# One visit's first product moved ahead of another's second pass, the first block's x put first in the queue, and a third of the attention loads issued by ScalarE

## The chip, the cores and the metric

The kernel runs on one core of a Trainium2 chip. The core has five engines that run their own instruction streams and wait for each other by semaphores: TensorE (PE; its weight loads are listed as PEld), VectorE (DVE), ScalarE (ACT), GpSimd (POOL) and SyncE (SP), which here only issues DMAs. Within one engine the instructions run in the order in which the program wrote them. The metric is the device time of one execution in microseconds (us); lower is better. The kernel before takes 867.36 us (median of 3 runs, 867.32 to 869.23).

## The reference

An attention over short bands, and behind it a mixture of four dense experts that all work on every row.

```python
B, H, S, D = 4, 8, 576, 64          # attention
scores = q @ k.T / sqrt(D)
# heads 0-3: keys within 32 positions back; heads 4-7: every 4th of the last 128
attn = softmax(masked scores); x = (attn @ v) -> (2304, 512)
# experts: E = 4, D = 512, F = 1024
p = probs / sum(probs)
out = sum over e of p[:, e] * (relu(x @ w1[e]) @ w2[e])
```

All inputs and the output are float32.

## The kernel before

**Attention.** The work is cut into groups of one batch, one pair of heads and three blocks of 64 queries. Batch 0 has 12 steps of one group, batches 1 to 3 have 6 steps each of two groups. A step's life is a pipeline over the loop `for n in range(len(steps) + LAG)`: `s_qk` (PE, tile `sc`) and `s_max` (DVE, tile `sm` and `nm`) in turn n, `s_sub` (POOL) and `s_exp` (ACT) one turn later, `s_sum` (DVE) and `s_norm` (POOL) two, `s_tr` (PE transposes into `pt`, then a copy to `pts`) three, `s_av` (PE, tile `po`, then ACT copies it into the row tile `xr`) four turns later. At the head of each turn `load_qk` and `load_v` issue the DMAs of groups to come; each has 6 buffers, so a load waits until the group six before it has been used. All of them stand in SP's queue, with the loads of the expert weights (`r`, lines 98 and 106).

**Experts.** A float32 operand is split into a rounded high part and a rest (`split`, lines 113 and 116: ACT writes the high part, POOL or DVE the rest), and a product takes three matmuls per 128 rows: high by high, rest by high, high by rest. A *visit* (u, m) is slice u of the experts' hidden columns (256 of them, 16 slices in all) on row block m (768 rows, 3 blocks; block 0 is batch 0 and the first third of batch 1; its x parts are made in two halves). In a visit the first layer is done in seven products instead of eight (a Strassen scheme): `mm1_a` makes A11 B11 and A12 B21, `mm1_b` makes S2 T2, S1 T1, S3 T3, S4 B22, A22 T4. The S are sums of weight blocks (POOL, `w1_sums`, tile `r`, lines 141 to 147, then split by `w1_late` into `g2h` and `g2l`), the T are sums of x blocks (DVE, `x_sums`, line 203, then split by `x_part` into `xh_...` and `xl_...`). A product is six matmuls of 384 columns into the bank `x` (`m1x` in the profile) or `y` (`m1y`). Their results pass through ACT and DVE (`s`, `u`, lines 418 to 441) to relu and split (`hh` by ACT at line 399, `hl` by DVE at line 405). `mm2` is the second layer: per 128 rows six matmuls of 512 columns into a tile `m`, two with `hl`, and DVE adds the result, weighted, to the accumulator (`acc`, line 486). It runs in two halves of 3 row tiles: half 1 uses h12 and h22 of this visit, half 0 uses h11 and h21.

**What sets the order.** The generator `experts` gives out PE's work piece by piece; up to 12 pieces are put between two turns of the attention. After each piece one or two items are taken from lists of small jobs (`queue`, `later`: splits, sums, x parts). `prepare` appends a job; `need` runs everything in a list up to the job that is asked for. The first visit (0, 0) is done without Strassen (`plain`): half 0 first, then it pauses until the attention has reached turn `OPEN` (20), then half 1. Until turn 14 (`START`) dummy matmuls (`wt`, line 671) fill in. The order of a visit's pieces in the kernel before is

```
mm1_b(this visit), mm2(this visit, half 1), mm1_a(next visit), mm2(this visit, half 0)
```

In the first 374 us attention and experts are mixed; after that only experts remain, with two buffers for each of `x` and `y` and four for `m` (before that one each and two).

Of the kernel before, what the change touches and what calls it, by code (L numbers as in the profile page):

```python
# [17 lines left out]
GB = 3  # L18
# [24 lines left out]
def kernel(  # L43
# [74 lines left out]
    def w1_split(u):  # L118

        r = raw1[u]  # L120
        gh = wp.tile([128, 3, 2, 128], F32R, tag="g1h", name="g1h", bufs=2)
        gl = wp.tile([128, 3, 2, 128], F32R, tag="g1l", name="g1l", bufs=2)
        a11, a12 = r[:, 0:2, 0:128], r[:, 2:4, 0:128]
        a21, a22 = r[:, 0:2, 128:256], r[:, 2:4, 128:256]
        for i, a in enumerate((a11, a12, a22)):
            split(gh[:, i], gl[:, i], a, nc.scalar, nc.gpsimd if u > 1 else nc.vector)
            a_op[u, ("A11", "A12", "A22")[i]] = (gh[:, i], gl[:, i])
            yield
        if u == 0:
            gh, gl = (wp.tile([128, 4, FU], F32R, tag=t, name=t) for t in ("g2h", "g2l"))  # L130
            v = (slice(None), slice(0, 2), slice(128, 256))
            split(gh[v], gl[v], a21, nc.scalar, nc.vector)
            a_op[u, "A21"] = (gh[v], gl[v])
# [86 lines left out]
    def attention(ap, xrp, pa):  # L220
# [27 lines left out]

        def load_v(b, p, gi):
            v_s = ap.tile([KB, 2, GB, 64], F32, tag="v", name="v_s", bufs=6)  # L250
            nc.sync.dma_start(out=v_s, in_=vw[b, p][:, :, gi * GB:(gi + 1) * GB, :])
            v_t[b, p, gi] = v_s

        def s_qk(n, gs):
# [67 lines left out]
        def s_tr(n, gs):  # L322
            sm = st[n]
            outs = []
            for k in range(len(gs)):
                pt = pa.tile([128, 512], F32, tag="pa", name="pt")
                for i in range(GB):
                    nc.tensor.transpose(  # L328
                        pt[:KB, i * 128:(i + 1) * 128], sm[:, k * GB + i, :KB], ident
                    )  # L330
                ts_ = ap.tile([KB, GB * 128], F32, tag="pts", name="pts", bufs=2)
                if k:
                    nc.vector.tensor_copy(ts_, pt[:KB, :GB * 128])
                else:
                    nc.scalar.activation(out=ts_, in_=pt[:KB, :GB * 128], func=AF.Copy)
                outs.append(ts_)
            st[n] = outs
# [75 lines left out]

    def mm1_a(k):
        u, m = k
        x, z, s1 = bank("x"), bank("y"), tmp("s1")
        product(x, u, "A11", m, "B11", True)
        nc.scalar.activation(out=s1, in_=x, func=AF.Copy)  # L418
        yield
        product(z, u, "A12", m, "B21", True)  # L420
        nc.vector.tensor_tensor(out=s1, in0=z, in1=s1, op=ALU.add)  # L421
        h_out(k, "11", s1, 2)
        st[k] = x
        yield
# [73 lines left out]
    def experts(begin):  # L498

        for half in range(2):  # L500
            for n in ("X12", "B22") if half else ("B11", "B21"):
                for i in range(2):
                    need(x_part, i, n)
            need(w1_split, 0)
            yield from plain((0, 0), half)
            if half == 1:
                for n, js in (("T4", (1, 0)), ("T3", (1,)), ("T1", (1,)), ("T2", (1,))):
                    for j in js:
                        prepare(x_part, j, n, soon=True)
                prepare(w1_late, 1, soon=True)  # L510
                prepare(w1_split, 2)
                prepare(w1_sums, 2)
            need(w2_late, 0)
            yield from mm2((0, 0), True, False, half)
            if half == 0:
                yield from pause("open")
            else:
                prepare(w2_late, 2)
        need(w1_split, 1)
        yield from mm1_a(visits[0])  # L520
        for i, (u, m) in enumerate(visits):
# [13 lines left out]
            if m == blocks[-1] and u + 2 <= LAST:  # L535
                prepare(w1_split, u + 2)
                prepare(w1_sums, u + 2)
            if m == blocks[0]:
                need(w2_late, u)
            yield from mm2((u, m), *ends, 1)  # L540
            if i + 1 < len(visits):
                begin()
                need(w1_split, visits[i + 1][0])
                need_x(visits[i + 1][1], ("B11", "B21"))
                yield from mm1_a(visits[i + 1])
                if visits[i + 1] == (NU - 1, 0):

                    need(x_sums, 5)
                    for n in ("T2", "T1"):
                        for j in (4, 5):  # L550
                            prepare(x_part, j, n)
# [30 lines left out]
    with tc.manual_schedule():  # L582
# [108 lines left out]
            when.setdefault(n, []).append((i, names))  # L691

        flat = [g for s in steps for g in s]
        qk_done = av_done = qk_next = v_next = 0

        dummies(18)
        ffn = experts(begin)
        for n in range(len(steps) + LAG):
# [14 lines left out]
                av_done += len(steps[n - LAG])  # L713
            for i, names in when.get(n, ()):
                for name in names:
                    of = queue if i < 2 else later
                    if name is None or name == "T2":
                        prepare(x_sums, i, of=of)
                    if name is not None:
                        prepare(x_part, i, name.upper(), of=of)  # L720
            if n == 6:
                fetch_w1(0)
            if n == 8:
# [92 lines left out]
```

## Time and profile before

| | |
|---|---|
| median of the runs | 867.36 us (3 runs) |
| the profiled execution's own time | 869.94 us |
| its span, first to last instruction | 868.2 us |
| mean granted TensorE clock | 0.987 of full speed |
| PE busy | 840.4 us (97%), 5096 matmul records |
| DVE, POOL, ACT busy | 504.9, 418.7, 328.4 us |
| chain that ended last, share of PE | 86% |

PE is busy 97% of the span, but its matmuls are pipelined and their ends modelled, so the gaps that are listed are a little shorter than what they cost. The table by stages in the rows below is to be read first: from 380 to 840 us PE never stands, and most of the 28 us in which it does lie before that. A row of the timeline gives the start, the duration and, in brackets, how long the engine had been idle before it and what released it.

### The profile page before, as it was taken

How to read it: one execution, taken by the hardware profiler on the slowest of the kernel's cores; microseconds unless marked ns; L12 is line 12 of the kernel's file. 1: busy time of each engine (PE TensorE's matmuls, PEld its weight loads, DVE VectorE, ACT ScalarE, POOL GpSimd, SP SyncE). 2: the span in 40 equal slices, each digit the busy share in tenths (PEclk: the TensorE clock that was granted, in tenths of full speed). 3: DMA queues.
4: the chain of work that ended last, by engine and by line, in shares of the span. 5: the costliest groups of instructions: out<-in, count | busy, mean ns of one | idle time of the engine just before them, and what ended most of it. 6: DMA issues, size and time to landing. Idle time of an engine off the chain costs nothing.

```text
span 868.2 us, 13457 instructions
## 1 busy us (share of the span) xinstructions
PE 840.4 (97%) x5096; PEld 733.1 (84%) x5096; DVE 504.9 (58%) x1046; ACT 328.4 (38%) x771; POOL 418.7 (48%) x491
## 2 busy tenths in 40 slices
PE   9697899999999999999999999999999999999998
PEld 6476688887888888888988989889898898988987
DVE  4677766568665568755455554555555555555454
ACT  4434544445344444533323422333333332333221
POOL 4557887677766678844323423422432332342210
PEclk9798999999999999999999999999999999999999
DMA  7862223322222211321001001010100100100003
GB/s 189 226 183 80 74 91 120 103 83 83 76 63 87 74 49 51 124 69 49 24 25 50 25 25 49 27 47 25 49 25 25 49 25 25 49 25 25 1 28 118
DMA packets 54528, 56.77 MB, mean 65 GB/s; under 512 B 5952, under 2 KB 43840, under 8 KB 54464
## 3 DMA queue, kind: packets, MB, share of 16 engines
q1 hardware_dynamic: 54464, 55.92, 21.0%
q8 instruction: 40, 0.66, 0.3%
q14 instruction: 24, 0.20, 0.1%
HBM read 51.19 MB, written 4.72 MB: 64 GB/s over the span
## 4 chain that ended last, share of the span: by engine, by line
PE 86%; DVE 7%; POOL 3%; ACT 2%; DMA 2%; issue 1%; SPq 0%; POOLq 0%; DVEq 0%; ACTq 0%
PE m L478 43%; PE m1x L381 22%; PE m1y L381 16%; DVE hl L405 3%; PE sc L263 1%; PE pt L328 1%; PE po L348 1%; DMA k_s<-kT 1%; DMA r<-w 1%; DVE xr L203 1%; DVE u L441 1%; PE wt L671 1%; DVE sm L277 1%; ACT hh L399 1%; ACT xh_T L113 0%
## 5 line engine op out<-in xcount | busy, mean ns | idle before, releaser
L486 DVE SCALAR_TENSOR_TENSOR acc<-m,pn,acc 128x512 f32<-128x512 f32 x270 | 201.8, 749 | 96.6 <-PE m L478 95.1
L478 PE MATMUL m<-w2h,hh 128*128 128x512 f32 x576 | 227.2, 394 | 3.2 <-DVE acc L486 2.5
L116 POOL TENSOR_TENSOR g2l<-r,g2h 128x256 fp32r<-128x256 f32 x124 | 92.7, 767 | 282.9 <-PE m L478 195.7
L478 PE MATMUL m<-w2l,hh 128*128 128x512 f32 x576 | 225.8, 392 | 0.0
L478 PE MATMUL m<-w2h,hl 128*128 128x512 f32 x576 | 182.4, 394 | 4.5 <-DVE hl L405 4.4
L478 PEld LDWEIGHTS m<-w2h,hl 128*128 128x128 f32 x576 | 108.0, 188 | 34.2 <-DVE hl L405 10.6
L478 PEld LDWEIGHTS m<-w2h,hh 128*128 128x128 f32 x576 | 108.1, 188 | 30.1 <-DVE acc L486 5.1
L478 PEld LDWEIGHTS m<-w2l,hh 128*128 128x128 f32 x576 | 108.2, 188 | 17.9
L116 POOL TENSOR_TENSOR w2l<-r,w2h 128x512 fp32r<-128x512 f32 x62 | 80.9, 1325 | 45.4 <-ACT w2h L113 45.2
L418 ACT ACTIVATE s<-m1x 128x384 f32<-128x384 f32 x47 | 23.1, 492 | 175.5 <-PE m1x L381 175.5
L437 DVE TENSOR_TENSOR s<-m1x,s 128x384 f32<-128x384 f32 x47 | 26.2, 558 | 103.9 <-PE m1x L381 102.6
L399 ACT ACTIVATE hh<-s 128x384 fp32r<-128x384 f32 x94 | 49.4, 526 | 98.1 <-DVE s L437 51.3
L116 POOL TENSOR_TENSOR g1l<-r,g1h 128x256 fp32r<-128x256 f32 x90 | 66.8, 757 | 36.2 <-ACT g1h L113 36.2
L430 ACT ACTIVATE u<-m1x 128x384 f32<-128x384 f32 x47 | 23.1, 492 | 146.8 <-PE m1x L381 146.8
L405 DVE SCALAR_TENSOR_TENSOR hl<-s,hh 128x384 fp32r<-128x384 f32 x94 | 59.6, 634 | 28.4 <-ACT hh L399 28.4
L421 DVE TENSOR_TENSOR s<-m1y,s 128x384 f32<-128x384 f32 x47 | 26.2, 557 | 61.1 <-PE m1y L381 58.3
L381 PE MATMUL m1x<-xh_T,g2h 128*128 128x384 f32 x156 | 52.8, 339 | 0.6 <-ACT u L430 0.3
L381 PE MATMUL m1x<-xl_T,g2h 128*128 128x384 f32 x156 | 52.6, 337 | 0.2 <-DVE xl_T L116 0.2
L381 PE MATMUL m1x<-xh_T,g2l 128*128 128x384 f32 x156 | 52.4, 336 | 0.0
L113 ACT ACTIVATE g2h<-r 128x256 fp32r<-128x256 f32 x125 | 45.2, 406 | 0.0
L381 PE MATMUL m1y<-xl_B,g2h 128*128 128x384 f32 x128 | 43.4, 339 | 0.0
L381 PE MATMUL m1y<-xh_B,g2h 128*128 128x384 f32 x128 | 43.4, 339 | 0.0
(92 smaller groups left out, 1584.8 us busy)
## 6 DMA issues: line engine op xcount, KB each, us to landing
r<-w SPq DMA_DIRECT2D x64, 512.0 KB, 3.5
v_s<-vw SPq DMA_DIRECT2D x48, 144.0 KB, 3.2
k_s<-kT SPq DMA_DIRECT2D x48, 112.0 KB, 3.1
q_s<-qT SPq DMA_DIRECT2D x48, 96.0 KB, 3.0
out<-acc SPq DMA_DIRECT2D x18, 256.0 KB, 2.0
mask<-masks SPq DMA_DIRECT2D x1, 288.0 KB, 2.9
pw<-probs SPq DMA_DIRECT2D x1, 36.0 KB, 4.5
```

The lines of the kernel that those rows point to most:

```text
L113: nc.scalar.activation(out=hi, in_=src, func=AF.Copy)
L116: lo_eng.tensor_tensor(out=lo, in0=src, in1=hi.bitcast(F32), op=ALU.subtract)
L203: nc.vector.tensor_tensor(out=quarter(i, d), in0=quarter(i, a), in1=quarter(i, b), op=ALU.subtract)
L381: nc.tensor.matmul(bank, w[:, k], x[:, k], start=(first and k == 0 and i == 0), stop=(last and k == 1 and i == 2), skip_group_check=True,)
L399: nc.scalar.activation(out=hi, in_=src, func=AF.Relu)
L405: nc.vector.scalar_tensor_tensor(out=lo, in0=src, scalar=0.0, in1=hi.bitcast(F32), op0=ALU.max, op1=ALU.subtract)
L418: nc.scalar.activation(out=s1, in_=x, func=AF.Copy)
L421: nc.vector.tensor_tensor(out=s1, in0=z, in1=s1, op=ALU.add)
L430: nc.scalar.activation(out=u2, in_=x, func=AF.Copy)
L437: nc.vector.tensor_tensor(out=s5, in0=x, in1=s5, op=ALU.add)
L478: nc.tensor.matmul(po, h, w, start=(n == 0 and x == 0), stop=(n == 3))
L486: nc.vector.scalar_tensor_tensor(out=acc, in0=po, scalar=pn[:, tt, e:e + 1], in1=acc, op0=ALU.mult, op1=ALU.add,)
```

## The change

It has five parts.

1. `load_v` of batches 0 and 1 is issued by ScalarE's queue instead of SyncE's (24 of 48 loads).
2. The copy of the second group's transposes (`pts`) is done by ACT instead of DVE in the six steps of batch 1.
3. The x parts of block 0 that a turn prepares are put at the head of the list `queue` instead of its end. With it, in half 1 of the first visit, the split and the sums of w1 slice 1 are called for before the T parts are prepared.
4. The rest parts of w1 slice 1 (`g1l`, three of them) are made by POOL instead of DVE.
5. `mm1_a` makes A12 B21 first (into `y`, ACT copies it), and A11 B11 after it (into `x`, DVE adds it). The next visit's A12 product is put ahead of this visit's `mm2` half 1, its A11 product stays behind it; the calls of `begin`, `need(w1_split)` and `need_x` move ahead with it.

```diff
--- before.py
+++ after.py
@@ -123,7 +123,7 @@
         a11, a12 = r[:, 0:2, 0:128], r[:, 2:4, 0:128]
         a21, a22 = r[:, 0:2, 128:256], r[:, 2:4, 128:256]
         for i, a in enumerate((a11, a12, a22)):
-            split(gh[:, i], gl[:, i], a, nc.scalar, nc.gpsimd if u > 1 else nc.vector)
+            split(gh[:, i], gl[:, i], a, nc.scalar, nc.gpsimd if u else nc.vector)
             a_op[u, ("A11", "A12", "A22")[i]] = (gh[:, i], gl[:, i])
             yield
         if u == 0:
@@ -248,7 +248,8 @@
 
         def load_v(b, p, gi):
             v_s = ap.tile([KB, 2, GB, 64], F32, tag="v", name="v_s", bufs=6)
-            nc.sync.dma_start(out=v_s, in_=vw[b, p][:, :, gi * GB:(gi + 1) * GB, :])
+            queue = nc.scalar if b < 2 else nc.sync
+            queue.dma_start(out=v_s, in_=vw[b, p][:, :, gi * GB:(gi + 1) * GB, :])
             v_t[b, p, gi] = v_s
 
         def s_qk(n, gs):
@@ -329,7 +330,7 @@
                         pt[:KB, i * 128:(i + 1) * 128], sm[:, k * GB + i, :KB], ident
                     )
                 ts_ = ap.tile([KB, GB * 128], F32, tag="pts", name="pts", bufs=2)
-                if k:
+                if k and gs[k][0] > 1:
                     nc.vector.tensor_copy(ts_, pt[:KB, :GB * 128])
                 else:
                     nc.scalar.activation(out=ts_, in_=pt[:KB, :GB * 128], func=AF.Copy)
@@ -413,12 +414,13 @@
 
     def mm1_a(k):
         u, m = k
-        x, z, s1 = bank("x"), bank("y"), tmp("s1")
+        z, s1 = bank("y"), tmp("s1")
+        product(z, u, "A12", m, "B21", True)
+        nc.scalar.activation(out=s1, in_=z, func=AF.Copy)
+        yield
+        x = bank("x")
         product(x, u, "A11", m, "B11", True)
-        nc.scalar.activation(out=s1, in_=x, func=AF.Copy)
-        yield
-        product(z, u, "A12", m, "B21", True)
-        nc.vector.tensor_tensor(out=s1, in0=z, in1=s1, op=ALU.add)
+        nc.vector.tensor_tensor(out=s1, in0=x, in1=s1, op=ALU.add)
         h_out(k, "11", s1, 2)
         st[k] = x
         yield
@@ -504,6 +506,8 @@
             need(w1_split, 0)
             yield from plain((0, 0), half)
             if half == 1:
+                need(w1_split, 1)
+                need(w1_sums, 1)
                 for n, js in (("T4", (1, 0)), ("T3", (1,)), ("T1", (1,)), ("T2", (1,))):
                     for j in js:
                         prepare(x_part, j, n, soon=True)
@@ -535,14 +539,18 @@
             if m == blocks[-1] and u + 2 <= LAST:
                 prepare(w1_split, u + 2)
                 prepare(w1_sums, u + 2)
+            if i + 1 < len(visits):
+
+                begin()
+                need(w1_split, visits[i + 1][0])
+                need_x(visits[i + 1][1], ("B11", "B21"))
+                opening = mm1_a(visits[i + 1])
+                yield next(opening)
             if m == blocks[0]:
                 need(w2_late, u)
             yield from mm2((u, m), *ends, 1)
             if i + 1 < len(visits):
-                begin()
-                need(w1_split, visits[i + 1][0])
-                need_x(visits[i + 1][1], ("B11", "B21"))
-                yield from mm1_a(visits[i + 1])
+                yield from opening
                 if visits[i + 1] == (NU - 1, 0):
 
                     need(x_sums, 5)
@@ -691,6 +699,7 @@
             when.setdefault(n, []).append((i, names))
 
         flat = [g for s in steps for g in s]
+        first_x = []
         qk_done = av_done = qk_next = v_next = 0
 
         dummies(18)
@@ -713,11 +722,13 @@
                 av_done += len(steps[n - LAG])
             for i, names in when.get(n, ()):
                 for name in names:
-                    of = queue if i < 2 else later
+                    of = first_x if i < 2 else later
                     if name is None or name == "T2":
                         prepare(x_sums, i, of=of)
                     if name is not None:
                         prepare(x_part, i, name.upper(), of=of)
+            queue[:0] = first_x
+            first_x.clear()
             if n == 6:
                 fetch_w1(0)
             if n == 8:
```

**SyncE and ScalarE in the single-group steps** (q_s, k_s, v_s are the load buffers, r1 the raw w1 slice, xr, pts and sm the attention tiles). SyncE before:

```order
L245 DMA q_s_281<-qT 128x192
L246 DMA k_s_282<-kT 128x224
L251 DMA v_s_285<-vw 96x2x192
L245 DMA q_s_322<-qT 128x192
L246 DMA k_s_323<-kT 128x224
L251 DMA v_s_326<-vw 96x2x192
L245 DMA q_s_362<-qT 128x192
L246 DMA k_s_363<-kT 128x224
L251 DMA v_s_366<-vw 96x2x192
L98 DMA r1_400<-w1 128x4x256
```

SyncE in the change, at the same place:

```order
L245 DMA q_s_281<-qT 128x192
L246 DMA k_s_282<-kT 128x224
L245 DMA q_s_322<-qT 128x192
L246 DMA k_s_323<-kT 128x224
L245 DMA q_s_362<-qT 128x192
L246 DMA k_s_363<-kT 128x224
L98 DMA r1_400<-w1 128x4x256
```

The v loads of the same groups stand in ScalarE's queue in the change, each ahead of the copies of its turn:

```order
L302 ACTIVATE sm0_94<-sm0_94 128x3x96
L252 DMA v_s_326<-vw 96x2x192
L365 ACTIVATE xr_299<-po_333 128x4x48
L336 ACTIVATE pts_345<-pt_341 96x384
L302 ACTIVATE sm1_95<-sm1_95 128x3x96
L252 DMA v_s_366<-vw 96x2x192
L365 ACTIVATE xr_299<-po_373 128x4x48
L336 ACTIVATE pts_385<-pt_381 96x384
```

SyncE has two issues per group where it had three, and ScalarE one more in each turn.

**ScalarE at the start of half 1 of the first visit** (turn 20; xh_T4 from xr_930 and xh_B22 are the second halves of the x parts that this half multiplies, xh_T2, T1, T3 are for the visit after it, g1h, w2h and g2h are weight splits of slice 1). Before:

```order
L113 ACTIVATE xh_T2_0_1278<-xr_299 128x2x192
L113 ACTIVATE xh_T1_0_1282<-xr_299 128x2x192
L113 ACTIVATE xh_T3_0_1286<-xr_299 128x2x192
L113 ACTIVATE g1h_1290<-r1_617 128x256 x3
L113 ACTIVATE w2h_1302<-r2_683 128x512 x2
L113 ACTIVATE xh_T4_0_883<-xr_930 128x2x192
L113 ACTIVATE xh_B22_0_887<-xr_930 128x2x192
L399 ACTIVATE hh_1337<-m1x_1315 128x384
L399 ACTIVATE hh_1348<-m1y_1316 128x384
```

In the change:

```order
L113 ACTIVATE xh_T4_0_883<-xr_930 128x2x192
L113 ACTIVATE xh_B22_0_887<-xr_930 128x2x192
L400 ACTIVATE hh_1305<-m1x_1283 128x384
L400 ACTIVATE hh_1316<-m1y_1284 128x384
L113 ACTIVATE xh_T2_0_1320<-xr_299 128x2x192
L113 ACTIVATE xh_T1_0_1324<-xr_299 128x2x192
L113 ACTIVATE xh_T3_0_1328<-xr_299 128x2x192
L113 ACTIVATE g1h_1332<-r1_617 128x256 x3
L113 ACTIVATE w2h_1344<-r2_683 128x512
L113 ACTIVATE g2h_1356<-r1_617 128x2x128 x4
```

The two x parts have moved from behind eight copies to the front, and those copies now stand behind the two `hh`, which wait for the products of this half. POOL takes its work at this place from those copies; in the change its order is

```order
L116 TENSOR_TENSOR xl_T2_0_1321<-xr_299,xh_T2_0_1320 128x2x192
L116 TENSOR_TENSOR xl_T1_0_1325<-xr_299,xh_T1_0_1324 128x2x192
L116 TENSOR_TENSOR xl_T3_0_1329<-xr_299,xh_T3_0_1328 128x2x192
L116 TENSOR_TENSOR g1l_1333<-r1_617,g1h_1332 128x256 x3
L141 TENSOR_TENSOR r1_617<-r1_617 128x2x128
L143 TENSOR_TENSOR r1_617<-r1_617 128x2x128
L145 TENSOR_TENSOR r1_617<-r1_617 128x2x128
L147 TENSOR_TENSOR r1_617<-r1_617 128x2x128
L116 TENSOR_TENSOR w2l_1345<-r2_683,w2h_1344 128x512
L116 TENSOR_TENSOR g2l_1357<-r1_617,g2h_1356 128x2x128 x4
```

where before the row of the three `g1l` is missing (DVE made them) and both `w2l` stand ahead of `g2l`.

**TensorE at the end of a visit on block 0** (m1x and m1y are the banks x and y, g1h and g1l the split of A22 and then of A12, m2 the second layer). Before:

```order
L381 MATMUL m1x_1590<-xh_T4_0_883,g1h_1419 128x384
L381 MATMUL m1x_1590<-xh_T4_0_883,g1l_1420 128x384
L381 MATMUL m1x_1590<-xl_T4_0_884,g1h_1419 128x384
L478 MATMUL m2_1796<-w2h_1571,hh_1775 128x512
L478 MATMUL m2_1796<-w2l_1572,hh_1775 128x512
L478 MATMUL m2_1796<-w2h_1571,hh_1780 128x512
L478 MATMUL m2_1796<-w2l_1572,hh_1780 128x512
L478 MATMUL m2_1796<-w2h_1571,hl_1778 128x512
L478 MATMUL m2_1796<-w2h_1571,hl_1782 128x512
```

In the change:

```order
L382 MATMUL m1x_1599<-xl_T4_0_884,g1h_1428 128x384
L382 MATMUL m1y_1796<-xh_B21_0_739,g1h_1656 128x384
L382 MATMUL m1y_1796<-xh_B21_0_739,g1l_1657 128x384
L382 MATMUL m1y_1796<-xl_B21_0_740,g1h_1656 128x384
L480 MATMUL m2_1806<-w2h_1580,hh_1775 128x512
L480 MATMUL m2_1806<-w2l_1581,hh_1775 128x512
L480 MATMUL m2_1806<-w2h_1580,hh_1780 128x512
L480 MATMUL m2_1806<-w2l_1581,hh_1780 128x512
L480 MATMUL m2_1806<-w2h_1580,hl_1778 128x512
L480 MATMUL m2_1806<-w2h_1580,hl_1782 128x512
```

Six matmuls of the next visit (three rows, each twice) have come between the last product of this visit and the matmul that reads `hl`; the number of matmuls is the same.

## Rows read from the trace of the kernel before

**Rows 1.** Busy time of each engine by stretch, with granted clock and DMA share

```profile
core 0: us, PE busy (x) PEld busy (x) DVE busy (x) ACT busy (x) POOL busy (x), PEclk, DMA share, GB/s
...
32.00:40.00 8.00, 4.83 (x47) 3.12 (x47) 4.39 (x28) 3.52 (x8) 6.00 (x6) 0.59 0.78 225
40.00:48.00 8.00, 7.00 (x54) 6.07 (x57) 2.02 (x14) 0.56 (x2) 2.25 (x2) 0.56 0.85 253
...
100.00:380.00 280.00, 271.88 (x1744) 233.82 (x1743) 183.93 (x356) 128.48 (x312) 207.79 (x231) 1.00 0.26 83
380.00:840.00 460.00, 460.00 (x2304) 415.20 (x2303) 239.99 (x384) 148.28 (x336) 150.90 (x187) 1.00 0.10 32
```

**Rows 2.** Waits of PE: us in total, times, longest us

```profile
PE m1x L381 <- ACT xh_T L113: 4.6, 2, 4.4
PE m L478 <- DVE hl L405: 4.4, 10, 0.5
PE sc L263 <- DMA k_s<-kT: 3.6, 3, 2.5
...
PE po L348 <- DVE pts L333: 0.3, 1, 0.3
```

**Rows 3.** Timeline of SP's DMA issues: start us, us, what

```profile
12.81 1.61 SPq L251 DMA_DIRECT2D v_s<-vw  x1
...
16.25 0.54 SPq L245 DMA_DIRECT2D q_s<-qT  x1
16.83 0.43 SPq L246 DMA_DIRECT2D k_s<-kT  x1
17.30 0.57 SPq L251 DMA_DIRECT2D v_s<-vw  x1
```

**Rows 4.** Timeline of all engines, 24 to 42 us; idle before and releaser in brackets

```profile
29.73 0.63 ACT L113 ACTIVATE w2h<-r 128x512 fp32r<-128x512 f32 x1 [1.33 <-DMA r<-w]
...
31.01 0.57 PE L348 MATMUL po<-pts,v_s 96*64 96x64 f32 x12 [0.80 <-ACT pts L335]
...
32.53 0.53 PE L328 MATMUL pt<-ident,sm 128*96 128x128 f32 x3 [0.95 <-POOL sm L316]
```

**Rows 5.** Timeline of all engines, 12 to 20 us: ScalarE's copies of one turn

```profile
15.90 0.33 ACT L364 ACTIVATE xr<-po 128x192 f32<-128x192 f32 x1 [0.48 <-PE po L348]
...
16.41 0.49 ACT L335 ACTIVATE pts<-pt 96x384 f32<-96x384 f32 x1 [0.18 <-PE pt L328]
```

**Rows 6.** Timeline of all engines, 134.5 to 140.5 us: a visit's end

```profile
136.21 0.34 PE L381 MATMUL m1x<-xh_T,g1h 128*128 128x384 f32 x1
...
136.41 0.56 DVE L441 TENSOR_TENSOR u<-m1y,u 128x384 f32<-128x384 f32 x1 [0.41 <-PE m1y L381]
...
137.28 0.39 PE L478 MATMUL m<-w2h,hh 128*128 128x512 f32 x1
...
137.91 1.09 DVE L405 SCALAR_TENSOR_TENSOR hl<-u,hh 128x384 fp32r<-128x384 f32 x1
...
138.20 0.40 PE L478 MATMUL m<-w2h,hl 128*128 128x512 f32 x1
...
139.06 0.50 PE L478 MATMUL m<-w2h,hl 128*128 128x512 f32 x1 [0.47 <-DVE hl L405]
```

**Rows 7.** Timeline of ACT, 56 to 96 us

```profile
69.58 1.33 ACT L113 ACTIVATE xh_T<-xr 128x384 fp32r<-128x384 f32 x3
```

**Rows 8.** Timeline of PE, 60 to 100 us

```profile
73.33 0.69 PE L381 MATMUL m1x<-xh_T,g1h 128*128 128x384 f32 x1 [4.35 <-ACT xh_T L113]
...
87.53 0.44 PE L381 MATMUL m1x<-xh_T,g2h 128*128 128x384 f32 x1 [0.25 <-ACT xh_T L113]
```

**Rows 9.** Timeline of POOL, 56 to 96 us

```profile
70.16 3.09 POOL L116 TENSOR_TENSOR xl_T<-xr,xh_T 128x384 fp32r<-128x384 f32 x3
73.95 0.97 POOL L141 TENSOR_TENSOR r<-r 128x256 f32<-128x256 f32 x1 [0.70 <-DVE g1l L116]
...
77.91 2.83 POOL L116 TENSOR_TENSOR w2l<-r,w2h 128x512 fp32r<-128x512 f32 x2
80.97 2.17 POOL L116 TENSOR_TENSOR g2l<-r,g2h 128x256 fp32r<-128x256 f32 x3 [0.23 <-ACT g2h L113]
```

## The prediction

> **What bounds the kernel now.** I read the busy time by stages first. From 380 to 840 us PE is busy 460.00 of 460 us; from 100 to 380 us 271.88 of 280 [rows 1]. Nothing that the change does to the late stage can shorten it, unless it adds a wait: the matmuls are the same in number. What can be had lies in the gaps of the first 380 us, so I read PE's waits second, sorted by total. Three sums matter: 4.6 us for an x part from ACT (nearly all of it one wait of 4.35 us), 4.4 us in ten waits for `hl` from DVE, and 3.6 us in three waits for a k load [rows 2]. Third, the granted clock: 0.59 and 0.56 in the stretches 32 to 40 and 40 to 48 us [rows 1], so much of that stretch ran at 1.2 GHz instead of 2.4, after PE had stood repeatedly between 31 and 34 us [rows 4]. The change has a part for each of these.
>
> **Part 1, v loads from ScalarE.** In the single-group steps SP spends 0.54 + 0.43 + 0.57 us on the three issues of a group, and with the gaps a group takes it from 16.25 to about 17.98, so 1.73 us [rows 3]. Nothing waits on SP there except the loads themselves, but there is no room for the four weight loads and the table of probabilities, and some issues take longer (1.61 us at 12.81). Without v a group costs it about 1.0 us. The k loads that PE waited for should then be in time. I count the whole 3.6 us [rows 2]. The w2 load, which stands behind them on SP, also comes earlier: ACT waited 1.33 us for it, and behind that wait stood the copy that PE's `po` at 31.01 missed (0.80 us idle) and, by way of POOL, the `pt` at 32.53 (0.95) [rows 4]. I count both, 1.75 us. The lower end of these two sums is nothing at all, or a little below nothing, if the early q, k and mask loads now share the transfer engines with three v loads issued beside them; I allow 1 us.
>
> What it costs: each issue sits on ACT. In a turn ACT is idle 0.48 us before the `xr` copy and 0.18 us before `pts` [rows 5], together 0.66, against one issue of 0.57 us as on SP [rows 3]. It just fits, so I cost it at nothing, but with 0.09 us of room. If the issue must wait for an older transfer, `xr`, `pts` and the exponential queue behind it, and PE's next `po` waits for `pts`. That is a rival below.
>
> The Trainium skill speaks against this part: its page "DMA: Bandwidth & Descriptors", section "Issuing engines are not separate DMA queues", says that loads started from different engines run on the same 16 DMA engines, and that only the time to start them is saved, usually small beside the transfer. Here that time is not small, since three issues fill 1.73 us per group; but the DMA share of 0.78 to 0.85 from 32 to 48 us [rows 1] says that the engines have little room either. By the rule the 3.6 and 1.75 us would stay.
>
> **The clock.** From 32 to 48 us PE is busy 4.83 + 7.00 us at mean clocks of 0.59 and 0.56 [rows 1]. A mean of 0.59 between the two levels is (1 - 0.59) / 0.5 = 82% of the time at the low one, 0.56 is 88%. So 0.82 x 4.83 + 0.88 x 7.00 = 10.1 us of PE's work ran at half speed, and 5.0 us would be saved if it ran at full speed. Whether the clock stays up depends on the gaps that are left between 24 and 34 us, of which part 1 removes some. And some of the gain would be given back: a faster PE meets the attention's chain on DVE and POOL, which had time then (DVE 2.02 of 8 us busy from 40 to 48). Between 0 and 5.0 I take 2.5.
>
> **Part 2, `pts` by ACT.** One copy less on DVE in six steps. By the list PE waited 0.3 us for it in all (`po` for DVE's `pts`) [rows 2]; I count that, from 0 to 1.
>
> **Parts 3 and 4, block 0's x first.** The wait of 4.35 us ends when the x part of half 1 arrives at 73.33 [rows 8]. ACT began its row of x copies at 69.58, but with T parts and weight splits for the next visit [rows 7]. With the two parts in front PE could start near 70.2, that is 3.1 us earlier. But the eight copies that were in front are now behind two `hh`, and these wait for the products of half 1. I follow POOL, which has to make what comes next. Half 1's 24 first-layer matmuls take four times 1.07 us (a product from 136.21 to 137.28 [rows 6]), to 74.5; two `hh`, then the first T copy on ACT, to 75.5. From there POOL's order is three `xl_T` (3.09), three `g1l`, which DVE made before (2.17, as three `g2l` of the same size), four sums (73.95 to 77.91, so 3.96), one `w2l` (half of 2.83) and the first `g2l` (0.72) [rows 9]: 11.4 us, to 86.9. S2 T2, the first product of the next visit that needs this `g2l`, began at 87.53 before [rows 8]. So of 3.1 us only 0.6 is left there, because the chain on POOL ran under the long wait and now starts after it. PE would arrive near 81.2 (75.0, then 18 matmuls of the second layer at 0.23, then two products) and stand over 5 us, longer than the 4.35 us after which the clock fell last time, so the fall moves with it. On the other side the T parts are further ahead, and two or three short waits behind 87.53 go. I count 0, from -3 (clock low over more work) to 4.4 (the whole wait gone).
>
> **Part 5, A12 ahead.** In the visits on block 0 PE reads `hl` as the fifth matmul of half 1. The five from 137.28 to 138.20 start 0.23 apart, the next at 139.06: 0.63 us lost (0.47 listed as idle) since `hl<-u` began at 137.91 and took 1.09 [rows 6]. There are ten of these [rows 2], so 6.3 us. The A12 product puts 1.07 us between, more than any of them, and `hl` needs nothing from it. What can it wait for itself? Bank y: the add at 136.41 that reads it ends at 136.97, 0.3 us before A12 would start at 137.28 [rows 6]. And its weight split, which stands one visit ahead in the lists. A11's result is added by DVE instead of copied by ACT, then has the 4 us of half 0 before x is written again. I count 6.3, from 0 to 7.
>
> **The sum.** 3.6 + 1.75 + 2.5 + 0.3 + 0 + 6.3 = 14.45 us. The profiled execution took 869.94 us (span 868.2 and 1.74 around it), 2.58 above the median of the runs, 867.36. Its gaps are taken to be the median's too, so the change comes to 867.36 - 14.45 = 852.9, say **853 us**. Nothing after 380 us takes it back, as PE has no idle time there in which to lose it.
>
> **Rivals.**
> - *The transfers come no earlier* (the shared DMA engines bound them). For: DMA share of 0.85. Against: 225 and 253 GB/s in those stretches [rows 1] while SP is what feeds them. Parts 1 and the clock give nothing; 0.3 + 6.3 = 6.6 is left: 860.8 us.
> - *The opening pays too.* The 4.35 us wait goes without a new one, if POOL's chain is shorter than the sum above or the splits are not late: 14.45 + 4.4 = 18.9, 848.5 us. Against: POOL's order, which the change itself lays down.
> - *A12 meets bank y or a late split*, and the ten waits only change their name: 14.45 - 6.3 = 8.15, 859.2 us. Against: 0.3 us of room at 136.97.
> - *ScalarE is held by the loads, slower.* The place is ACT's queue in the 18 steps of batches 0 and 1. It decides from an issue that takes more than the 0.66 us of idle time per turn. An issue like SP's of 1.61 us is 0.95 too long; in 15 of the 18 steps that is 14.2 us, with the low clock at the opening (3) 17.2, against the 6.6 that parts 2 and 5 give: +10.6, 878 us. Against: SP's ordinary issue is 0.57.
>
> **How the numbers follow.** The forecast has 0.59, transfers no earlier 0.15, the opening pays 0.13, A12 waits 0.07, ScalarE held 0.06. Forecast's own range, from the clock (2.5 either way) and the opening: 848 to 858. For 8 in 10 the range takes in the first two rivals: **846 to 862**. A measurement of this kernel can tell 0.3%, 2.6 us. Faster by more than that: the first four, 0.94, less 0.05 for sums of several low ends that come out at nothing: 0.89. Same 0.05. Slower 0.06.
>
> **What would show it.** Right: no wait of PE for k loads, the clock at 1.00 from 32 to 48 us, half 0's first m1 matmul 5 to 8 us earlier than in the kernel before; no wait of `m` for `hl` from 100 to 374 us; the first matmul of half 1 less than 1.5 us after the attention's last, and a new wait of 4 to 6 us before the first `g2h` product, with POOL busy through it. Wrong: ACT idle behind a v issue with `pts` late; a wait of m1y for `u`; PE idle after 380 us.

## The result and the profile after

The changed kernel takes 858.99 us (median of 4 runs, 857.71 to 859.81) against 867.34 us for the kernel before (median of 4, 866.63 to 869.23): a ratio of 0.9891, 95% interval 0.9868 to 0.9914, so 9.5 us less by the ratio (7.5 to 11.4) and 8.35 us less by the medians. The forecast was 853 us, 14.45 less. The direction was right. The time is inside the range of 846 to 862, but outside the forecast's own 848 to 858: the gain is 58% of what was summed by the medians, 66% by the ratio. The profiled execution took 858.22 us, with a span of 856.4.

The busy times by stages (columns as in [rows 1]) show where it came from:

```profile
32.00:40.00 8.00, 6.61 (x96) 5.39 (x97) 6.99 (x44) 3.88 (x10) 6.58 (x7) 1.00 0.83 257
40.00:48.00 8.00, 7.44 (x100) 6.07 (x99) 6.36 (x34) 5.19 (x12) 6.52 (x7) 1.00 0.67 178
72.00:80.00 8.00, 2.77 (x14) 2.11 (x14) 2.69 (x4) 2.84 (x8) 7.69 (x10) 0.94 0.00 0
80.00:100.00 20.00, 19.47 (x126) 17.07 (x126) 13.39 (x30) 11.11 (x28) 18.16 (x19) 0.85 0.29 89
300.00:320.00 20.00, 17.93 (x82) 15.68 (x81) 10.32 (x16) 8.63 (x21) 13.49 (x15) 0.91 0.20 58
380.00:840.00 460.00, 460.00 (x2300) 416.14 (x2299) 242.22 (x384) 144.58 (x330) 148.21 (x184) 1.00 0.10 33
```

From 32 to 48 us the clock is at 1.00 in this execution, where it was 0.59 and 0.56 [rows 1], and the late stage is untouched. Two places are worse than they should be: PE is busy 2.77 of 8 us from 72 to 80, and from 300 to 320 us there is a new hole of 2.07 us with a lower clock behind it. The list of PE's waits (us in total, times, longest) names both:

```profile
PE m1x L382 <- DVE s L423: 4.9, 1, 4.9
PE m L480 <- DVE acc L488: 3.0, 2, 1.7
PE pt L329 <- POOL sm L317: 2.7, 4, 1.2
PE m1y L382 <- DVE hl L406: 2.1, 1, 2.1
...
PE m1x L382 <- ACT xh_T L113: 1.1, 1, 1.1
```

Of the three sums of [rows 2], the k loads are gone, the ten waits of `m` for `hl` are gone, and the 4.35 us for the x part is 1.1. In their place stand 4.9 us for an `s` of DVE and 2.1 us of `m1y` for `hl`. The first is the wait that the forecast had put before the first `g2h` product. In the timeline of PE (start, duration, idle before and releaser):

```profile
62.47 0.44 PE L382 MATMUL m1x<-xh_T,g1h 128*128 128x384 f32 x1 [1.13 <-ACT xh_T L113]
...
79.81 0.66 PE L382 MATMUL m1x<-xh_T,g2h 128*128 128x384 f32 x1 [4.94 <-DVE s L423]
80.26 0.52 PE L382 MATMUL m1x<-xh_T,g2l 128*128 128x384 f32 x1
```

and POOL through it, beside DVE's adds and x parts:

```profile
68.28 2.96 POOL L116 TENSOR_TENSOR xl_T<-xr,xh_T 128x384 fp32r<-128x384 f32 x3 [5.89 <-ACT xh_T L113]
71.20 2.12 POOL L116 TENSOR_TENSOR g1l<-r,g1h 128x256 fp32r<-128x256 f32 x3
73.40 0.74 POOL L141 TENSOR_TENSOR r<-r 128x256 f32<-128x256 f32 x1
...
77.73 3.74 POOL L116 TENSOR_TENSOR g2l<-r,g2h 128x256 fp32r<-128x256 f32 x4
```

```profile
77.56 0.63 DVE L116 TENSOR_TENSOR xl_T<-xr,xh_T 128x384 fp32r<-128x384 f32 x1 [4.55 <-ACT xh_T L113]
78.35 0.84 DVE L116 TENSOR_TENSOR xl_T<-xr,xh_T 128x384 fp32r<-128x384 f32 x1 [0.15 <-ACT xh_T L113]
79.11 0.55 DVE L423 TENSOR_TENSOR s<-m1x,s 128x384 f32<-128x384 f32 x1
```

```profile
75.78 1.33 ACT L113 ACTIVATE g2h<-r 128x256 fp32r<-128x256 f32 x4 [5.32 <-POOL r L145]
```

POOL idles 5.89 us under half 1 and then works almost without a gap; its first `g2l` ends near 78.7. DVE's add that frees the bank x stands behind two T parts, whose copies on ScalarE stand behind the `g2h` copies, and these wait for POOL's sums. Both ways come out of the same chain. The distance from the start of the wait before half 1 to S2 T2 is 79.81 - (62.47 - 1.13) = 18.47 us; before it was 87.53 - (73.33 - 4.35) = 18.55 [rows 8]. The opening gave nothing, as forecast; that two effects cancel there is shown below, where parts 3 and 4 are undone.

### The profile page after: what moved, and what is told of

Read it like the earlier page. It is cut to its first block, busy times and chain, and to the rows that moved or that the text cites. A ratio compares the mean times of both kernels' runs of the same rounds, so it can differ in the third digit from the quotient of the medians.

```text
span 856.4 us, 13489 instructions
## 1 busy us (share of the span) xinstructions
PE 833.1 (97%) x5096; PEld 735.0 (86%) x5096; DVE 501.1 (59%) x1037; ACT 329.2 (38%) x777; POOL 420.2 (49%) x494
## 4 chain that ended last, share of the span: by engine, by line
PE 91%; DVE 4%; POOL 1%; ACT 1%; DMA 1%; issue 1%; SPq 0%; ACTq 0%; DVEq 0%; POOLq 0%
PE m L480 44%; PE m1x L382 23%; PE m1y L382 17%; PE po L349 2%; PE sc L264 2%; PE pt L329 2%; PE wt L679 1%; DMA k_s<-kT 1%; DVE acc L488 1%; DVE hl L406 1%; DVE xr L203 1%; DVE xl_T L116 1%; DVE sm L278 1%; POOL xl_T L116 0%; ACT hh L400 0%
## 5 line engine op out<-in xcount | busy, mean ns | idle before, releaser
L480 PE MATMUL m<-w2h,hl 128*128 128x512 f32 x576 | 178.6, 391 | 0.0
L116 POOL TENSOR_TENSOR g1l<-r,g1h 128x256 fp32r<-128x256 f32 x93 | 69.0, 757 | 65.3 <-ACT g1h L113 65.3
L113 ACT ACTIVATE g2h<-r 128x256 fp32r<-128x256 f32 x125 | 43.4, 405 | 6.0 <-POOL r L145 6.0
L382 PE MATMUL m1y<-xh_B,g2l 128*128 128x384 f32 x128 | 42.9, 335 | 0.0
L113 ACT ACTIVATE w2h<-r 128x512 fp32r<-128x512 f32 x64 | 38.5, 621 | 0.0
```

Of the source, the lines that this page charges most:

```text
L113: nc.scalar.activation(out=hi, in_=src, func=AF.Copy)
L116: lo_eng.tensor_tensor(out=lo, in0=src, in1=hi.bitcast(F32), op=ALU.subtract)
L382: nc.tensor.matmul(bank, w[:, k], x[:, k], start=(first and k == 0 and i == 0), stop=(last and k == 1 and i == 2), skip_group_check=True,)
L480: nc.tensor.matmul(po, h, w, start=(n == 0 and x == 0), stop=(n == 3))
```

## The experiments

Each kernel was timed in several rounds against the kernel before on the same chip; ratios are to that. The kernel before ran at medians of 869.02, 868.62 and 868.70 us there. The changed kernel was timed in a round of its own, where the kernel before took 867.34 us; so a distance from the changed kernel is given by the medians and, as the better measure, by the difference of the two ratios, times 868 us.

**Part 5 alone.** The kernel before with the new `mm1_a` and the A12 product ahead; the other four parts left out.

```diff
+            if i + 1 < len(visits):
+                begin()
...
+                opening = mm1_a(visits[i + 1])
+                yield next(opening)
             yield from mm2((u, m), *ends, 1)
             if i + 1 < len(visits):
-                begin()
...
-                yield from mm1_a(visits[i + 1])
+                yield from opening
```

> The kernel before with part 5 alone (A12 ahead, and with it the opening of the second set of banks). Theory A, the ten waits go but the opening of the later banks, which moved ahead with A12, now costs a wait of about 2 us and the low clock behind it: against before, 6.3 us less for the ten waits and about 3.9 more, so 2.4 us less, some 865 us; in its trace no wait of m for hl between 100 and 374 us, and one wait of m1y for the last hl near 320 us with the granted clock low just behind it. Rival B, the 3.9 us belong to another part and part 5 gives its whole 6.3: 861 us, and no such wait.

Measured: 863.79 us, ratio 0.9937 (0.9925 to 0.995), 5.5 us less. Its waits of PE:

```profile
PE m1x L381 <- DVE s L438: 2.4, 1, 2.4
...
PE m1y L381 <- DVE hl L405: 2.1, 1, 2.1
PE m1x L381 <- DVE s L422: 1.6, 1, 1.6
```

The wait of `m1y` for `hl` comes with part 5 alone. Theory A had this wait and a gain of 2.4 us, rival B no such wait and 6.3; the 5.5 us (4.3 to 6.5) are nearer to B's. So the place is right, and the two sizes are not yet told apart. Nor is the clock low just behind this wait, as theory A had it: it is 1.00 from 300 to 320 us and 0.91 from 320 to 340, behind a second hole, the row of 2.4 us:

```profile
333.87 0.44 PE L381 MATMUL m1x<-xh_T,g1h 128*128 128x384 f32 x1 [2.36 <-DVE s L438]
```

```profile
330.23 3.12 DVE L203 TENSOR_TENSOR xr<-xr 128x384 f32<-128x384 f32 x3
333.27 0.55 DVE L438 TENSOR_TENSOR s<-m1x,s 128x384 f32<-128x384 f32 x1
```

`begin()` does a second thing: it puts the x parts and sums of the last block into the list `later`. Called earlier, it let DVE make three of these sums ahead of the add that frees bank x. This profiled execution was the slowest of its six (865.41 us). The row of 1.6 us is another cost of this part: at the opening A11 now directly precedes S2 T2, which writes the same bank x.

**The later banks opened where they were.** The changed kernel, with `begin()` back behind the second layer's half 1.

```diff
             if i + 1 < len(visits):
-                begin()
                 need(w1_split, visits[i + 1][0])
...
             if i + 1 < len(visits):
+                begin()
                 yield from opening
```

> The changed kernel with only the opening of the later banks put back behind the second layer's half 1; A12 stays ahead. Theory A: the wait of 2.07 us at 310.87 and the half-speed matmuls behind it go, 3.9 us less than the changed kernel, so about 855 us, granted clock 1.00 from 300 to 340 us. Rival B: A12 at this place waits for something else (a weight split, the reader of bank y), and the wait stays under another name: no difference.

Measured: 855.15 us, ratio 0.9843 (0.9828 to 0.9857), 3.8 us under the changed kernel (4.2 by the ratios). The stretch from 300 to 320 us:

```profile
300.00:320.00 20.00, 20.00 (x100) 17.71 (x99) 12.23 (x18) 9.54 (x24) 13.21 (x17) 1.00 0.23 79
```

The hole and the low clock are gone, and the wait of `m1x` for `s` one visit later is 0.5 us instead of 1.0. (The low clock does not follow the hole in every execution: with part 2 undone, and with parts 3 and 4 undone, both below, the same wait is 2.1 us and the clock is 1.00 from 300 to 320 us.) In the changed kernel's trace the wait ends with the last reader of the other bank:

```profile
307.42 0.34 PE L382 MATMUL m1y<-xl_B,g2h 128*128 128x384 f32 x1
...
310.87 0.46 PE L382 MATMUL m1y<-xh_B,g1h 128*128 128x384 f32 x1 [2.07 <-DVE hl L406]
311.15 0.50 PE L382 MATMUL m1y<-xh_B,g1l 128*128 128x384 f32 x1
...
312.10 0.52 PE L382 MATMUL m1y<-xh_B,g1l 128*128 128x384 f32 x1
```

```profile
307.79 0.56 DVE L443 TENSOR_TENSOR u<-m1y,u 128x384 f32<-128x384 f32 x1 [0.41 <-PE m1y L382]
...
310.27 0.54 DVE L406 SCALAR_TENSOR_TENSOR hl<-m1x,hh 128x384 fp32r<-128x384 f32 x1
```

Bank y's own last reader, the add `u`, ended at 308.35; A12 started at 310.87, after `hl` from bank x ended at 310.81. `begin()` closes the attention's banks and lays new ones over them, so the first product in the new set waits for readers of the old one. Behind the half 1 matmuls that wait was covered.

**Part 5 alone, later banks where they were.** The kernel of the first experiment with that same edit.

> The kernel before with part 5 alone, but with the opening of the later banks left behind the second layer's half 1. Theory: part 5's two effects add up, so this is faster than the kernel with part 5 alone by what the banks cost in the changed kernel (3.8 us), 9 us faster than before: about 860 us. By the forecast's term it would be 6.3 us faster than before.

Measured: 859.80 us, ratio 0.9898 (0.9881 to 0.9915), 8.9 us less than before (7.4 to 10.3). So A12 ahead is worth about 9, not 6.3, and the moved call of `begin` takes 3.4 (by the ratios) to 4 (by the medians) of it back: the wait of 2.07 and, in the profiled executions, 2.36 - 0.50 = 1.86 at the second hole. By its trace, the stretch from the first S2 T2 to the end of the span is 857.3 - 86.60 = 770.7 us, 780.7 before (868.2 - 87.53 [rows 8]): 10 us less, and 1.3 are lost at the opening (19.9 us from the wait before half 1 to S2 T2, 18.55 before), the wait for bank x. The ten waits for `hl` are 6.3 of the 10 at the forecast's 0.63 us each. But from one first S2 T2 to the next, the eight visits in which such a wait stands alone came out 0.67 to 0.78 us shorter, 0.74 on average, so 7.4 for ten. The first visit behind the opening is 1.4 us shorter; the rest is spread over small pieces up to 370 us and was not taken apart.

**Part 1 alone.** The kernel before with only the v loads of batches 0 and 1 on ScalarE. (They are 24 of the 72 q, k and v loads of these two batches; the title's third is a third of these.)

```diff
-            nc.sync.dma_start(out=v_s, in_=vw[b, p][:, :, gi * GB:(gi + 1) * GB, :])
+            queue = nc.scalar if b < 2 else nc.sync
+            queue.dma_start(out=v_s, in_=vw[b, p][:, :, gi * GB:(gi + 1) * GB, :])
```

> The kernel before with part 1 alone (v of batches 0 and 1 issued by ScalarE). Theory: the three waits of TensorE for a k load go and the attention of turn 19 ends about 5 to 6.5 us earlier than in the kernel before (67.4 to 68.7 us there), the clock at 32 to 48 us coming out high in some executions and low in others; the whole kernel 4 to 6 us faster than before. The forecast's terms for this part (3.6 + 1.75 + 2.5) make 7.85. Rival: the transfers come no earlier, no change.

Measured: 864.22 us, ratio 0.9952 (0.994 to 0.9965), 4.2 us less. The wait before half 1 starts at 68.60 - 4.35 = 64.25 us, 4.7 earlier. From 14 to 62 us the waits of PE in the kernel before are, beside the 3.6 us for k loads of [rows 2],

```profile
PE pt L328 <- POOL sm L316: 1.7, 2, 1.0
PE pt L328 <- DMA k_s<-kT: 1.0, 1, 1.0
PE po L348 <- ACT pts L335: 0.8, 1, 0.8
```

and with part 1 alone, where these two are all:

```profile
PE po L349 <- ACT pts L336: 2.0, 2, 1.7
PE pt L329 <- POOL sm L317: 1.9, 3, 0.8
```

The waits for k loads are gone, and 1.0 us more of them than the forecast counted. But the 0.80 us of `po` and the 0.95 of `pt`, which it counted as gone with them, are not: the wait for `pts` grew to 2.0 us, and the one for POOL's `sm` stayed. In all, 7.1 us of listed waits became 3.9, so 3.2 went, where 3.6 + 1.75 had been counted.

The clock did not stay up here:

```profile
24.00:32.00 8.00, 5.45 (x63) 3.77 (x63) 4.86 (x22) 5.37 (x16) 4.06 (x6) 0.73 0.98 219
32.00:40.00 8.00, 7.13 (x123) 5.31 (x122) 6.84 (x37) 5.00 (x12) 4.77 (x7) 0.84 0.73 225
```

The low stretch follows a gap on PE that the kernel before does not have, and ScalarE shows what made it (ACTq is its DMA issue):

```profile
22.19 0.45 ACT L302 ACTIVATE sm<-sm 128x288 f32<-128x288 f32 x1 [0.22 <-POOL sm L294]
24.56 0.58 ACTq L252 DMA_DIRECT2D v_s<-vw  x1
25.19 0.33 ACT L365 ACTIVATE xr<-po 128x192 f32<-128x192 f32 x1 [2.56 <-DMA r<-w]
25.41 0.48 ACT L336 ACTIVATE pts<-pt 96x384 f32<-96x384 f32 x1
```

```profile
25.95 0.57 PE L349 MATMUL po<-pts,v_s 96*64 96x64 f32 x12 [1.72 <-ACT pts L336]
```

ScalarE stood 2.56 us at the v issue until the w1 load had landed, with `xr` and `pts` queued behind it, and PE missed `pts` for 1.72 us. That is the mechanism of the forecast's last rival; at this size it cost PE time once, not in 15 steps. In the program's instruction lists the two loads wait on one completion counter, of which there are eight for all loads of SyncE and ScalarE:

```
SyncE    L98  DMA r_400<-w 128x4x256 [waits DMAHW1_49]
ScalarE  L252 DMA v_s<-vw 96x2x192   [waits DMAHW1_49]
```

**The weight loads of slice 0 from GpSimd**, to take them off these counters. This edit and the next are to the kernel with T parts early and banks late ("Both edits" below).

```diff
-        nc.sync.dma_start(
+        (nc.gpsimd if u == 0 else nc.sync).dma_start(
             out=r, in_=w1[e, :, s * FU:(s + 1) * FU].rearrange("(c p) f -> p c f", p=128)
```

(and the same for w2)

> The kernel with both edits, and the loads of w1 and w2 slice 0 issued by GpSimd instead of SyncE. Theory: the v issue that stood 1.2 to 2.7 us on ScalarE near 22 to 25 us stood for the landing of the w1 load, which uses the same completion counter eight loads earlier; from another queue the weight loads have other counters, so ScalarE's idle time before that xr copy falls under 0.7 us, the wait of po for pts near 25 us goes where it was, and the attention of turn 19 ends 1 to 2 us earlier than the 63.2 us seen in the middle: about 850 us. Rival: the loads themselves bound it, or GpSimd is held by issuing them, and the time stays at 851.4 us or is longer.

Measured: 852.62 us, ratio 0.9813 (0.98 to 0.9826); without the edit 0.9793 (0.9778 to 0.9808). Not faster. The theory was too narrow:

```profile
26.59 0.33 ACT L365 ACTIVATE xr<-po 128x192 f32<-128x192 f32 x1 [2.01 <-DMA k_s<-kT]
...
30.22 0.33 ACT L365 ACTIVATE xr<-po 128x192 f32<-128x192 f32 x1 [1.99 <-DMA k_s<-kT]
```

ScalarE stands about as long, now for k loads, and PE's `po` missed `pts` for 2.0 and 1.6 us behind it. Not the size of the w1 load makes the wait, but that the load issued eight earlier on the same counters must have landed, while loads land late: from 10 to 32 us the median v load took 3.3 us from issue to landing before and 4.5 us in the changed kernel (k: 3.3 and 4.1).

**Two turns of v loads back on SyncE.**

```diff
-            queue = nc.scalar if b < 2 else nc.sync
+            queue = nc.scalar if b < 2 and ahead[0] not in (8, 9) else nc.sync
```

(`ahead[0]` holds the turn in which the load is issued)

> The kernel with both edits, and the v loads of turns 8 and 9 issued by SyncE, those of the other turns of batches 0 and 1 by ScalarE as in the change. Theory: the issue that would wait for the w1 load then stands on SyncE, where nothing of the pipeline stands behind it but later loads: as with the one before, 0.5 to 1.5 us less than both edits alone. Rival: SyncE's later q and k loads come late by the same wait, and nothing is gained.

Measured: 850.34 us, ratio 0.9789 (0.9775 to 0.9802): lower than without the edit by 1.0 us in the medians and 0.3 by the ratios, and the intervals overlap almost wholly. Inconclusive.

**Parts 3 and 4 undone** in the changed kernel.

```diff
-                    of = first_x if i < 2 else later
+                    of = queue if i < 2 else later
...
-            split(gh[:, i], gl[:, i], a, nc.scalar, nc.gpsimd if u else nc.vector)
+            split(gh[:, i], gl[:, i], a, nc.scalar, nc.gpsimd if u > 1 else nc.vector)
```

(and without the calls of `need(w1_split, 1)` and `need(w1_sums, 1)`)

> The changed kernel with parts 3 and 4 undone: block 0's x parts at the end of the list again, w1 slice 1 not called for early, its rest parts on DVE. Theory: the wait before half 1 is back (about 4.4 us) and the one of 4.94 us before S2 T2 is gone or under 1 us, so the time is that of the changed kernel within 1.5 us. Rival: parts 3 and 4 paid after all, and it is 3 to 4.5 us slower than the changed kernel.

Measured: 859.75 us, ratio 0.9899 (0.9884 to 0.9914), against 0.9891 with them: 0.7 us, not to be told from nothing. Its waits of PE:

```profile
PE m1x L382 <- ACT xh_T L113: 4.3, 1, 4.3
...
PE m1x L382 <- DVE s L423: 1.6, 1, 1.6
```

The old wait is back, the new one is 1.6 instead of 4.9. The expectation of under 1 us was off by bank x. The opening in the timeline of PE:

```profile
67.94 0.69 PE L382 MATMUL m1x<-xh_T,g1h 128*128 128x384 f32 x1 [4.35 <-ACT xh_T L113]
...
83.51 0.41 PE L382 MATMUL m1x<-xh_T,g2h 128*128 128x384 f32 x1 [1.62 <-DVE s L423]
```

From the start of the wait before half 1 to S2 T2 it takes 83.51 - (67.94 - 4.35) = 19.92 us, and with parts 3 and 4 18.47. So they do shorten the opening, by 1.4 us, about what part 5 had added to it (1.3), and lose part of this again to the clock, as the low stretch covers 6.1 us of PE's work (79.8 to 85.9) instead of 4.5 (67.9 to 72.5).

**Part 2 undone** in the changed kernel (`if k:` again for `if k and gs[k][0] > 1:`).

> The changed kernel with part 2 undone: the second group's pts copy of batch 1 on DVE again. Theory: 0.3 us, from 0 to 1, not to be told from the changed kernel. Rival: DVE's copy holds up the maxima behind it in six turns, 2 us or more slower.

Measured: 859.93 us, ratio 0.9903 (0.9889 to 0.9916). Not to be told from the changed kernel (1.0 us by the ratios).

**T parts early.** The changed kernel with the jobs of slice 1, and the T parts that stand before them in the list, ahead of half 1.

```diff
             need(w1_split, 0)
-            yield from plain((0, 0), half)
             if half == 1:
                 need(w1_split, 1)
                 need(w1_sums, 1)
+            yield from plain((0, 0), half)
+            if half == 1:
                 for n, js in (("T4", (1, 0)), ("T3", (1,)), ("T1", (1,)), ("T2", (1,))):
```

> The changed kernel with the T parts of block 0's first half and the split and sums of w1 slice 1 called for ahead of half 1 instead of behind it, so that ScalarE and GpSimd do them while they stand idle from 62 to 66 and 62 to 68 us. Theory: GpSimd's chain of 10.4 us starts 5 us earlier, and the wait of 4.94 us before the first S2 T2 shrinks to 0 to 1.5, with no low clock behind it: 4 to 6 us less, 853 to 855 us. Rival: TensorE is then late on the copies of hh, which stand behind eight more copies on ScalarE, or on the second halves of the T parts, and the wait only moves: less than 1.5 us gained.

Measured: 855.11 us, ratio 0.9845 (0.9829 to 0.9862), 3.9 us under the changed kernel (4.0 by the ratios), just short of the expected 4 to 6 by the medians. PE's wait before S2 T2 is 1.5 us instead of 4.9: the chain on POOL was what PE stood for.

**Both edits.**

> The two edits before this together. If they are independent: 8 to 10 us less than the changed kernel, about 850 us. If both work through the same slack in the attention's chain, less than 6.

Measured: 851.35 us, ratio 0.9793 (0.9778 to 0.9808), 7.6 us under the changed kernel (8.5 by the ratios). The two edits add up: 3.8 and 3.9, by the ratios 4.2 and 4.0. The expected 8 to 10 is met by the ratios and missed by 0.4 us in the medians. PE's wait before S2 T2 and DVE ahead of it:

```profile
78.57 0.41 PE L382 MATMUL m1x<-xh_T,g2h 128*128 128x384 f32 x1 [1.47 <-DVE s L423]
```

```profile
65.55 4.95 DVE L203 TENSOR_TENSOR xr<-xr 128x384 f32<-128x384 f32 x4
```

**Both edits, and three more at the opening.**

```diff
+            second = mm2((0, 0), True, False, half)
+            if half == 1:
+                yield next(second)
+                yield from mm1_a(visits[0])
+            yield from second
...
+                for n in ("T1", "T2"):
+                    prepare(x_part, 1, n, soon=True)
+                queue.extend(held)
```

(`held` is the split of w2 slice 1, taken out of the list before half 1)

> The kernel with both edits (T parts early, banks late), and three more at the opening: A12 and A11 of visit (1, 0) between the first and the second row tile of the second layer's half 1, the T2 and T1 parts of the second half ahead of the S splits, and the w2 splits of slice 1 behind them. Theory: the first S2 T2 begins 1.4 us earlier than with both edits alone (GpSimd's first g2l, one w2l less ahead of it, then decides it), and the wait of 0.5 for T1 goes: 1.5 to 2 us less, about 849.5 us. Rival: the later w2 splits make the second layer of the next visit wait, or DVE's list is in another order than is good, and nothing is gained.

Measured: 851.52 us, ratio 0.9806 (0.9791 to 0.9821). Nothing gained. In its trace S2 T2 stands 77.98 - (65.63 - 1.15) = 13.5 us behind the start of the wait before half 1 instead of 15.2, but the waits for `acc` grow from 2.7 to 3.2 us and those for `hh` from 0.6 to 1.1, and the attention's stage ended 1 us later in this execution, the slowest of its four. Its clock is also 0.57 from 100 to 104 us, behind one of the waits for `acc`, where it is 1.00 with both edits alone.

## Why the prediction was partly right

- **Part 1 and the clock** (3.6 + 1.75 + 2.5 = 7.85): the mis-sized term, 4.2 us in the chip's timing (3.0 to 5.2). The k waits did go from the changed kernel's list, and half 0 began 5.5 us earlier in the profiled execution (36.67 instead of 42.16). But the sum counted 3.6 + 1.75 us of waits as gone, and by the lists of part 1 alone 3.2 went. The step that failed is the issue on ScalarE, costed at nothing because 0.57 us fitted into 0.66 of room per turn: its issues came to wait for older loads (2.56 us at 25.19), the loads landed later, and PE's wait for `pts` grew from 0.8 to 2.0 us instead of going. This price was bounded on the side of the rival and left out of the forecast; it should have been put in at one or two waits of 2 us. A rule of the Trainium skill was weighed there ("DMA: Bandwidth & Descriptors", section "Issuing engines are not separate DMA queues"): loads share the same 16 DMA engines whoever starts them, and only the time to start them is saved. The trace agrees with the first half, as the median v load took 4.5 us to land instead of 3.3. That the 3.6 us would therefore stay, as the forecast worked it out from the rule, did not come: the waits for k loads went.
- **The clock**: 2.5 was taken between 0 and 5. The changed kernel's one profile, with 1.00 from 24 to 48 us, would have confirmed the upper end. But in the ten traces with v loads on ScalarE the mean over these 24 us was 1.00 twice and 0.72 to 0.93 in the other eight; in the three without them it was 0.72, 0.64 and 0.79. On average that is 0.85 against 0.72, with ranges that overlap: the clock seems to fall less, but still falls in most executions, and one trace does not tell.
- **Part 2** (0.3): not to be told from nothing, as said.
- **Parts 3 and 4** (0): right in its place, and in its size with some luck. The stall moved, POOL busy through it. But beside part 5, which lost 1.3 us to bank x at the opening (not in the forecast), these parts gave 1.4 back there and lost part of it to the clock; the nothing is what is left of these. The end of POOL's chain was forecast for 11.4 us behind the first T copy and came after 10.4 (68.28 to 78.7); the clock fell with it.
- **Part 5** (6.3): the ten waits went as forecast, and none of them came back under another name. The term is off in two ways that partly cancel: 9 instead of 6.3 for A12 ahead (a wait for `hl` cost about 0.74 us and not 0.63, and the first visit became shorter too), and 3.4 to 4 taken back by waits that the forecast put at nothing; it had looked for them only at bank y and at a weight split. The text of the change named their cause: the call of `begin` moves ahead. It was read as bookkeeping, and what it does once, at the end of the attention, was not followed: it changes the bank sets (the wait of 2.07 us) and queues the last block's x jobs (the second hole). 5.5 us remain of part 5 as the change has it.
- **The sum**: 4.2 (part 1 with the clock) + 5.5 (part 5) = 9.7, with the others at nothing, against 9.5 measured by the ratio. The account closes within its intervals. That the measured 859 us is close to the 859.2 and 860.8 us of two rivals is chance: the ten waits did not change their name, and part 1 did give something.

## What to carry to other kernels

A load that is moved to a compute engine's queue puts every wait of its issue in front of that engine's work, and with transfers that land after 4 us the completion counters can be such a wait; count the landing time, not only the issue time. When a step is moved ahead, follow everything that its calls do, above all the opening and closing of buffer sets: a wait that was covered where it stood need not be where it goes. And where a chain on another engine ends a wait, starting that chain earlier (3.9 us here) pays, while reordering the work that waits for it gained nothing that could be measured.

## What the runs showed that was not expected

DVE and POOL slow each other when both work in SBUF, the on-chip memory that holds the x parts. Three x sums alone on DVE took 1.74 us in the changed kernel, with POOL idle:

```profile
63.49 1.74 DVE L203 TENSOR_TENSOR xr<-xr 128x384 f32<-128x384 f32 x3
```

With both edits four took 4.95 us beside POOL's x parts and the `g1l` behind them, so 1.24 each instead of 0.58, and POOL's three parts took longer too:

```profile
65.40 3.69 POOL L116 TENSOR_TENSOR xl_T<-xr,xh_T 128x384 fp32r<-128x384 f32 x3 [0.93 <-ACT xh_T L113]
```

That is 1.23 each instead of 0.99 (2.96 / 3). It is no single case: in the trace of both edits the two x sums with POOL idle took 0.54 us each, and the fourteen with POOL busy throughout 0.71 to 1.37. DVE's add `u`, which reads a bank and one SBUF tile, took 0.56 us either way. The Trainium skill, "SBUF — State Buffer", section "SBUF: two separate sides", says that the two share a port pair as an exclusive lock, for a DVE operation with two inputs in SBUF against one of GpSimd that reads SBUF. The trace agrees that both lose, and that the add with one input in SBUF does not; but one operation of each after the other would take 0.58 + 0.99 = 1.57 us a pair, and the pair took 1.24, which is the figure to go by.
